# Lightning attention into a gated feed-forward: two-block tiles with one bank and one cosine for two w_in slices, fewer homes, and a last block in one piece

## The chip, the cores and the metric

The kernel runs on one core of a Trainium2 chip. The metric is the device time of a run in microseconds (us), lower is better. The times of the kernel before are 202.65, 202.12 and 202.6 us, median 202.6. Engines are named as in the profile: PE (TensorE matmuls), PEld (its weight loads), DVE (VectorE), ACT (ScalarE), POOL (GpSimd), SP (SyncE, which issues most DMAs); a name with a small q (SPq, ACTq) is an engine's sequencer.

## The reference

Two computations in a row. First a linear attention with decay: for 4 batches and 8 heads, in blocks of 64 positions, `intra = (qb @ kb.T * Dmask) @ vb`, `inter = (qb * lam_pow) @ kv_state`, `out = intra + inter`, and the state is carried on, `kv_state = lam_block * kv_state + kb_dec.T @ vb`. Its output, put in token order, is `x` of 3072 tokens by 512. Then a feed-forward:

```python
h = x @ w_in            # 512 -> 2048
g = h * np.cos(h)
return (g @ w_out).astype(np.float32)   # 2048 -> 512
```

## The kernel before, in words

The 3072 tokens are 24 blocks of 128 tokens. They are cut into eight tiles of 4, 2, 2, 2, 2, 4, 4 and 4 blocks (`TILES`). Attention works on pairs of blocks (pair `pr` is blocks `2 pr` and `2 pr + 1`); the feed-forward works on tiles.

**Feed-forward of a tile.** w_in's 2048 columns are 16 slices of 128, numbered f. For each slice four matmuls (L753) sum into one PSUM bank `ps_h`, 512 columns wide for a tile of four blocks and 256 for one of two. ACT takes the cosine out of the bank (L759), DVE multiplies bank and cosine into `g` (L765, the gating product), and then the bank is free. For each block, 16 matmuls with w_out (L800) sum into a bank `ps_f`; ACT copies it out (L816) into a home `o_sb`, and a DMA stores it (L823 or L825). The last block, 23, is done in two pieces of 384 and 128 columns: 16 matmuls each; DVE copies the first piece and SP stores it, ACT copies the second and stores it itself.

**Attention in visits.** While PE does a tile's feed-forward, it turns for short visits to the attention of later pairs. A full visit for pair `pr` is one uninterrupted row on PE: values that need no turn (L491, `ps_o`, two banks), the scores of the next pair (L429, `ps_s`, two banks), its state update (L441, `ps_kv`, two banks, and PE writes them in turn, matmul by matmul), the other values (L491) and the carried part (L523). Between the first and the other values stands a one-element DVE copy out of `ps_o` (L508, tile `spare`; called the turn copy here); it waits until the first values are done, and the other values wait for it. After the visit DVE multiplies scores with the mask (`s_m`, L434) and sums states (`sum`, L447), and ACT casts states (`S`, L451) and the attention output (`xT`, L531).

**Banks and homes.** PSUM has eight banks, and everything above shares them; a bank is taken again once its last reader is through. Outputs of blocks 0 to 11 are held back in SBUF until the key transposes of pair 10 have been issued on SP (`HELD`), since the loads of q, k and v fill the DMA queues until then. Before, these twelve have homes of their own (`o_held`, 12 buffers, which earlier hold parts of the start), and other outputs have three (`o_sb`). Raw q, k and v of a block each take one of six buffers (`ld`).

**Order.** Every engine's order is written out by a planner: tasks have durations, dependencies and a priority, and each engine takes, among the tasks that could start, the one of best priority. The turn copy has a priority ahead of everything and may make DVE wait for it up to 0.45 us of planned time although another task could start (`look.worth`). What the planner assumes sets the order alone; on the chip each engine runs its row in that order and waits where it must.

Of the kernel before, what the change touches and what calls it, by code (L numbers as in the profile page):

```python
# [10 lines left out]
F32 = mybir.dt.float32  # L11
BF16 = mybir.dt.bfloat16
# [18 lines left out]
HELD = (10,) * 12  # L31

# [30 lines left out]
class Planner:  # L63


    LAT = {"PE": 0.2, "ACT": 0.06, "DVE": 0.08, "POOL": 0.1, "SP": 0.0, "DMA": 0.0, "SETUP": 0.0}

# [10 lines left out]
    def order(self):  # L78
# [5 lines left out]
        while todo:  # L84
# [24 lines left out]
            free[t.eng] = t.end  # L109
# [44 lines left out]
def kernel(  # L154
# [30 lines left out]
    BUFS = {"ld": 6, "qk": 3, "v_s": 6, "qkT": 3, "s_m": 4, "cos": 3, "o_sb": 3, "o_held": 12}  # L185
# [55 lines left out]
    unit = [MM(n * P, 4 * KF) + MM(DM, KF * n) + ATT * n for n in TILES]  # L241
# [356 lines left out]
    span_v = [consts.tile([P, H, 2, D], BF16, name=f"v_sp{x}") for x in range(SPANS)]  # L598

    def add_span(x):  # L600
# [109 lines left out]
    def add_span_state(s_t, prio):  # L710
# [21 lines left out]
        u.bank_frees = [[x]]  # L732

    h_last, o_last = {}, {}
    hid, closing = [], None

    def add_ffn(i):
        nb, n0 = TILES[i], first[i]
        cols = nb * P
        gate = {}  # L740

        for f in range(KF):
            gate[f] = []
            blocks = [(0, 2), (2, 4)] if i == 0 and f < SPLIT else [(0, nb)]
            for b0, b1 in blocks:
                pr = begins[i] + (f + b0 / 4 * SPLIT) * unit[i] / KF
                at = slice(b0 * P, b1 * P)
                n = (b1 - b0) * P

                def hidden(task, f=f, at=at, n=n):  # L750
                    t = bank(task.bank[0], [P, 4 * P], F32, "ps_h")
                    live["h", i, f, at.start] = t
                    return [nc.tensor.matmul(t[:, :n], lhsT=w_in_sb[:, kd, f * P:(f + 1) * P],  # L753
                                             rhs=live["xT", i][:, kd, at], start=(kd == 0), stop=(kd == KD - 1))
                            for kd in range(KD)]

                def cosine(_, f=f, at=at, n=n):
                    c = work.tile([P, 4 * P], F32, tag="cos", bufs=BUFS["cos"], name="cos")
                    nc.scalar.activation(c[:, :n], live["h", i, f, at.start][:, :n], AF.Sin, bias=halfpi)  # L759
                    live["c", i, f, at.start] = c  # L760

                def gated(_, f=f, at=at, n=n):
                    if ("g", i) not in live:
                        live["g", i] = work.tile([P, KF, 4 * P], BF16, tag="g", name="g")
                    return nc.vector.tensor_mul(live["g", i][:, f, at], live.pop(("h", i, f, at.start))[:, :n],  # L765
                                                live.pop(("c", i, f, at.start))[:, :n])

                h = pl.add("PE", MM(n, 4), [x for m in range(n0 + b0, n0 + b1) for x in Vo[m]] + [w_t["in", next(c for c in range(len(W_IN)) if f < sum(W_IN[:c + 1]))]],
                           hidden, pr, banks=1)
                a = pl.add("ACT", 0.21 + n * 0.000833, [h], cosine, pr, get="cos")  # L770
                d = pl.add("DVE", 0.12 + n * 0.00104, [a] + ([o_last[i - 2]] if i >= 2 else []), gated, pr)
                h.bank_frees = [[d]]
                a.frees = [d]
                gate[f].append(d)
                if i == 0 and f == KF - 3:
                    pace.append(d)
                h_last[i] = h
                h.many = True
                if i == 0:
                    hid.append(h)  # L780
        nonlocal closing
        nxt = unit[i + 1] if i + 1 < len(unit) else unit[i]
        U4 = 4
        for j in range(nb):
            last = n0 + j == NBLK - 1
            tag = "o_held" if n0 + j < len(HELD) or i == len(TILES) - 1 else "o_sb"
            cuts = [0, 3 * DM // 4, DM] if last else [0, DM]
            pieces = [slice(a, z) for a, z in zip(cuts, cuts[1:])]
            store = None
            for piece, part in enumerate(pieces):  # L790
                width = part.stop - part.start
                for f0, nf in [(0, 4), (4, 4), (8, 4), (12, 2), (14, 2)] if i == 0 else [(f, U4) for f in range(0, KF, U4)]:
                    pr = begins[i + 1] + (j + f0 / KF) * nxt / nb + piece
                    if i == 0 and f0 >= KF - U4:
                        pr = begins[i + 1] + (3.75 + 0.05 * j + 0.1 * (f0 - 12)) * nxt / nb

                    def project(task, j=j, f0=f0, nf=nf, piece=piece, part=part, width=width):
                        if f0 == 0:
                            live["f", i, j, piece] = bank(task.bank[0], [P, DM], F32, "ps_f")
                        return [nc.tensor.matmul(live["f", i, j, piece][:, :width], lhsT=live["g", i][:, f, j * P:(j + 1) * P],  # L800
                                                 rhs=w_out_sb[:, f, part], start=(f == 0), stop=(f == KF - 1))
                                for f in range(f0, f0 + nf)]

                    t = pl.add("PE", MM(width, nf), [x for f in range(f0, f0 + nf) for x in gate[f]] + (w_last[f0 - 12:f0 - 12 + nf] if f0 >= KF - U4 else [w_t["out", f0 * WCH // KF]]) + [store],
                               project, pr, banks=0 if f0 else 1)
                    if i == 0 and j == nb - 1:
                        closing = t
                    t.many = True
                    if f0 == 0:
                        head = t  # L810
                    store = t
                o_last[i] = store

                def project_out(_, eng, j=j, piece=piece, width=width, tag=tag):
                    o = live["o_sb", i, j, piece] = work.tile([P, DM], F32, tag=tag, bufs=BUFS[tag], name="o_sb")
                    return (nc.scalar.copy if eng == "ACT" else nc.vector.tensor_copy)(o[:, :width], live["f", i, j, piece][:, :width])  # L816

                def store_out(_, eng, j=j, piece=piece, part=part, width=width):
                    b, c = where(n0 + j)
                    r0 = b * S + c * P  # L820
                    if n0 + j < 2 * SPANS:
                        for s, h in enumerate(halves):
                            nc.sync.dma_start(out=out[r0 + s:r0 + P:2, :], in_=live["o_sb", i, j, piece][h])  # L823
                        return
                    (nc.scalar if eng == "ACT" else nc.sync).dma_start(  # L825
                        out=out[r0:r0 + P, part], in_=live["o_sb", i, j, piece][:, :width])

                eng, queue = ("DVE", "SP") if last and piece == 0 else ("ACT", "ACT" if last else "SP")
                e = pl.add(eng, 0.12 + width / 1060.0, [store], partial(project_out, eng=eng), begins[i + 1] + (j + 1) * nxt / nb,
                           get=tag)  # L830
                d = dma(queue, 1.2 if n0 + j < 2 * SPANS else 0.9, 1.7 if n0 + j < 2 * SPANS else 0.75, partial(store_out, eng=queue), n0 + j + 8, [e] + ([T[HELD[n0 + j], 1].issue] if n0 + j < len(HELD) else []), ordered=False)[1]
                e.frees = [d]
                head.bank_frees = [[e]]
# [136 lines left out]
```

## Time and profile before

| | |
|---|---|
| runs, median (lowest, highest) | 202.6 us (202.12, 202.65) |
| profiled execution, first to last instruction | 200.7 us |
| of a run outside that span, 202.6 - 200.7 | 1.9 us |
| PE busy | 192.9 us, 96% |
| DVE, ACT, POOL busy | 112.1, 117.1, 64.9 us |
| first matmul of the dense part, end of the last | 16.84, 197.62 us |
| granted clock of TensorE | 1.000 |

The span is that of one execution under the profiler. The profile has no time of that execution from the host's side, so the 1.9 us between its span and the median of the runs is taken as a constant. Durations of matmuls (379 ns for 512 columns) are from issue to the modelled end; the pace of matmuls in a row is read from stretches (24 in 5.18 us are 0.216 us each).

### The profile page before, as it was taken

To read this page: it belongs to the slowest core of one execution; us is meant where nothing else is said; L and a number is where in the kernel's file an instruction comes from. 1 tells how busy PE (TensorE), PEld (TensorE's weight loads), DVE (VectorE), ACT (ScalarE), POOL (GpSimd) and SP (SyncE) were. 2 spreads that over 40 slices of the span, in tenths; PEclk is the share of its full clock that TensorE was granted. 3 is DMA by queue.
4 is the path that set the end of the run, shared out by engine and by line. 5 is a ranking of instruction groups with operands and counts; after the bars stand their busy time and mean duration, and the time that the engine had idled before them with its cause. 6 is when DMAs were issued, how large, how long until landed. Compare 5 with 4: busy or idle time off the path is not lost.

```text
span 200.7 us, 5731 instructions
## 1 busy us (share of the span) xinstructions
PE 192.9 (96%) x2380; PEld 110.2 (55%) x2407; DVE 112.1 (56%) x211; ACT 117.1 (58%) x223; POOL 64.9 (32%) x86
## 2 busy tenths in 40 slices
PE   8899999999999999999999999999999999999993
PEld 2466444648758647858755454544445444444452
DVE  2978772448848816956745679565445453444001
ACT  5878771329769527939555878486356465344120
POOL 5893002284373645472636570006400000000000
DMA  5999999999899999998999997999611010111112
GB/s 163 303 191 202 205 196 239 289 221 177 203 218 214 184 241 201 214 213 184 191 207 220 245 206 183 318 314 223 162 56 54 3 52 6 49 52 52 52 63 97
DMA packets 96668, 34.46 MB, mean 172 GB/s; under 512 B 84738, under 2 KB 93186, under 8 KB 96642
## 3 DMA queue, kind: packets, MB, share of 16 engines
q1 hardware_dynamic: 89664, 29.83, 66.6%
q0 software_dynamic: 6832, 4.20, 14.5%
q8 instruction: 19, 0.31, 0.7%
q10 hardware_dynamic: 146, 0.07, 0.1%
q14 instruction: 7, 0.06, 0.1%
HBM read 27.26 MB, written 6.29 MB: 167 GB/s over the span
## 4 chain that ended last, share of the span: by engine, by line
PE 89%; DMA 6%; issue 1%; SPq 1%; POOL 1%; ACT 0%; POOLq 0%
PE ps_f L800 41%; PE ps_h L753 41%; DMA sp_f<-in_k_dram 3%; DMA w_in_sb<-in_moe_w_in_dram 3%; PE ps_o L491 2%; PE ps_o L523 2%; PE ps_kv L441 2%; PE ps_s L429 1%; SPq L260 1%; POOL k_sp L614 1%; PE ps_t L381 0%; PE ps_kv L718 0%; PE ps_x L491 0%; ACT o_sb L816 0%; POOLq L614 0%
## 5 line engine op out<-in xcount | busy, mean ns | idle before, releaser
L765 DVE TENSOR_TENSOR g<-ps_h,cos 128x256 bf16<-128x256 f32 (+1 forms) x133 | 70.6, 543 | 41.4 <-ACT cos L759 39.7
L800 PE MATMUL ps_f<-w_out_sb,g 128*128 128x512 bf16 (+2 forms) x380 | 87.6, 370 | 2.2 <-issue 1.6
L753 PE MATMUL ps_h<-xT,w_in_sb 128*128 128x256 bf16 (+1 forms) x525 | 88.8, 319 | 0.5 <-issue 0.2
L759 ACT ACTIVATE cos<-ps_h,halfpi 128x256 f32<-128x256 f32 (+1 forms) x133 | 72.0, 570 | 28.9 <-PE ps_h L753 28.3
L753 PEld LDWEIGHTS <-w_in_sb 128*128 128x128 bf16 x532 | 51.4, 98 | 32.9 <-DMA w_in_sb<-in_moe_w_in_dram 0.4
L800 PEld LDWEIGHTS <-g 128*128 128x128 bf16 x400 | 37.6, 98 | 40.4
L351 POOL TENSOR_TENSOR qk<-q_f,q_scale 128x512 bf16<-128x512 f32 x19 | 19.4, 1042 | 54.2 <-DMA q_f<-in_q_dram 54.2
L816 ACT COPY o_sb<-ps_f 128x512 f32<-128x512 f32 (+1 forms) x24 | 13.7, 574 | 22.6 <-PE ps_f L800 19.6
L359 POOL TENSOR_TENSOR v_s<-v_f,v_scale 128x512 bf16<-128x512 f32 x19 | 19.6, 1043 | 9.2 <-DMA v_f<-in_v_dram 5.4
L531 ACT CAST xT<-ps_o 128x512 bf16<-128x512 f32 x15 | 8.1, 589 | 13.6 <-PE ps_o L523 11.2
L434 DVE TENSOR_TENSOR s_m<-ps_s,mask 128x512 bf16<-128x512 f32 x20 | 12.9, 685 | 2.5 <-PE ps_s L429 2.0
L355 POOL CAST qk<-k_f 128x512 bf16<-128x512 f32 x18 | 11.0, 612 | 7.8 <-DMA k_f<-in_k_dram 7.8
L447 DVE TENSOR_TENSOR sum<-sum,ps_kv 128x512 f32<-128x512 f32 x15 | 10.2, 682 | 0.7
L451 ACT CAST S<-sum 128x512 bf16<-128x512 f32 x15 | 9.1, 618 | 1.0 <-DVE sum L447 0.9
L508 DVE COPY spare<-ps_o 1x1 f32<-1x1 f32 x8 | 1.2, 156 | 14.6 <-PE ps_o L491 14.6
L816 DVE COPY o_sb<-ps_f 128x384 f32<-128x384 f32 x1 | 0.6, 558 | 11.6 <-PE ps_f L800 11.6
L491 PEld LDWEIGHTS <-v_s 64*64 64x64 bf16 x320 | 4.2, 106 | 4.4 <-issue 4.0
L491 PE MATMUL ps_o<-s_m,v_s 64*64 64x64 bf16 x288 | 5.9, 197 | 0.0
L638 DVE TENSOR_TENSOR s_m_sp<-ps_s,mask_sp 128x512 bf16<-128x512 f32 x8 | 5.1, 685 | 1.3 <-PE ps_s L633 1.3
L892 PE MATMUL ps_idle<-const-float32-1.0 128*128 128x512 f32 (+1 forms) x6 | 4.8, 902 | 0.8 <-PEq L954 0.8
L523 PE MATMUL ps_o<-qkT,S 64*64 64x64 bf16 x304 | 5.0, 195 | 0.0
L441 PE MATMUL ps_kv<-v_s,qk 64*64 64x64 bf16 x288 | 4.8, 195 | 0.0
(77 smaller groups left out, 83.9 us busy)
## 6 DMA issues: line engine op xcount, KB each, us to landing
q_f<-in_q_dram SPq DMA_DIRECT2D x20, 256.0 KB, 3.9
k_f<-in_k_dram SPq DMA_DIRECT2D x20, 256.0 KB, 4.5
v_f<-in_v_dram SPq DMA_DIRECT2D x20, 256.0 KB, 4.5
out_dram<-o_sb SPq DMA_DIRECT2D x19, 256.0 KB, 2.8
w_out_sb<-in_moe_w_out_dram POOLq DMA_DIRECT2D x3, 512.0 KB, 13.6
sp_f<-in_q_dram SPq DMA_DIRECT2D x2, 512.0 KB, 4.9
sp_f<-in_k_dram SPq DMA_DIRECT2D x2, 512.0 KB, 5.4
w_in_sb<-in_moe_w_in_dram POOLq DMA_DIRECT2D x2, 512.0 KB, 9.1
```

The source lines that it names most:

```text
L351: return vec[e].tensor_mul(new_qk()[:, 0, :, s], live.pop(("q_f", 2 * pr + s)), q_scale[:, c, :].unsqueeze(2).to_broadcast([P, H, D]))
L355: return (nc.scalar.copy if early else nc.gpsimd.tensor_copy)(new_qk()[:, 1, :, s], live.pop(("k_f", 2 * pr + s)))
L359: return vec[e].tensor_mul(live["v_s", 2 * pr + s], live.pop(("v_f", 2 * pr + s)), v_scale[:, c, :].unsqueeze(2).to_broadcast([P, H, D]))
L434: return nc.vector.tensor_mul(t, live["s", pr][s], mask.unsqueeze(1).to_broadcast([P, H, D]))
L447: return nc.vector.tensor_add(new, live["sum", pr, 0] if half else live["sum", pr - 1, 1], live["kv", pr][half])
L451: return nc.scalar.copy(new_S(pr, half), live["sum", pr, half])
L491: yield lambda h=h: nc.tensor.matmul(o[halves[h % 2], h // 2], lhsT=live["v_s", n0 + s][m, h, :], rhs=live["s_m", n0 + s][m, h, :], start= ...
L753: return [nc.tensor.matmul(t[:, :n], lhsT=w_in_sb[:, kd, f * P:(f + 1) * P], rhs=live["xT", i][:, kd, at], start=(kd == 0), stop=(kd == KD ...
L759: nc.scalar.activation(c[:, :n], live["h", i, f, at.start][:, :n], AF.Sin, bias=halfpi)
L765: return nc.vector.tensor_mul(live["g", i][:, f, at], live.pop(("h", i, f, at.start))[:, :n], live.pop(("c", i, f, at.start))[:, :n])
L800: return [nc.tensor.matmul(live["f", i, j, piece][:, :width], lhsT=live["g", i][:, f, j * P:(j + 1) * P], rhs=w_out_sb[:, f, part], start= ...
L816: return (nc.scalar.copy if eng == "ACT" else nc.vector.tensor_copy)(o[:, :width], live["f", i, j, piece][:, :width])
```

## The change

Five things, and a large part of the diff that is not run (`FAST` is an empty list, so `project_pairs` and `add_w_sums` are never called).

- In tiles of two blocks, slices f and f+8 go into the two halves of one bank: eight matmuls of 256 columns, then one cosine and one gating product of 512 columns for both. Tiles of four blocks keep a bank for each slice, in the order 0, 8, 1, 9 and so on; w_out matmuls of a block come in the order f = 0-3, 8-11, 4-7, 12-15.
- `ld` goes from six to four buffers for each of q, k and v.
- All outputs share eleven homes (`o`) in place of 12 + 3. With the outputs of blocks 0 to 10 held, the twelfth output (block 11) has a home only when the stores of block 0 have landed.
- Block 23 is one piece of 512 columns, copied by ACT and stored by SP.
- Some tiles of the start move to other buffers, and the planner lets an engine start its next task 0.05 to 0.1 us before the planned end of the last (`TAIL`), with slightly longer cosines and gating products.

```diff
+    TAIL = {"ACT": 0.1, "DVE": 0.09, "POOL": 0.05}
-            free[t.eng] = t.end
+            free[t.eng] = t.end - self.TAIL.get(t.eng, 0.0)
-    BUFS = {"ld": 6, "qk": 3, "v_s": 6, "qkT": 3, "s_m": 4, "cos": 3, "o_sb": 3, "o_held": 12}
+    BUFS = {"ld": 4, "qk": 3, "v_s": 6, "qkT": 3, "s_m": 4, "cos": 3, "o": 11, "cmb": 2, "SA": 2, "E": 2}
...
+        if i == 0:
+            groups = [([f], b, (f + b[0] / 4 * SPLIT) / KF) for f in range(KF) for b in ([(0, 2), (2, 4)] if f < SPLIT else [(0, nb)])]
+        elif nb == 4:
+            groups = [([f], (0, nb), (2 * (f % HF) + f // HF) / KF) for x in range(HF) for f in (x, x + HF)]
+        else:
+            groups = [([x, x + HF], (0, nb), 2 * x / KF) for x in range(HF)]
...
+                return [nc.tensor.matmul(t[:, x * n:(x + 1) * n], lhsT=w_in_sb[:, kd, f * P:(f + 1) * P],
+                                         rhs=live["xT", i][:, kd, at], start=(kd == 0), stop=(kd == KD - 1))
+                        for x, f in enumerate(fs) for kd in range(KD)]
...
+                nc.scalar.activation(c[:, :m], live["h", key][:, :m], AF.Sin, bias=halfpi)
...
+                g = h_tile()[:, fs[0]:fs[-1] + 1:HF, at]
+                x = lambda t: t[:, :m].rearrange("p (f n) -> p f n", f=len(fs))
+                return nc.vector.tensor_mul(g, x(live.pop(("h", key))), x(live.pop(("c", key))))
...
-            cuts = [0, 3 * DM // 4, DM] if last else [0, DM]
...
+            for f0, nf in [(0, 4), (4, 4), (8, 4), (12, 2), (14, 2)] if i == 0 else [(0, 4), (8, 4), (4, 4), (12, 4)]:
...
-                eng, queue = ("DVE", "SP") if last and piece == 0 else ("ACT", "ACT" if last else "SP")
+            e = pl.add("ACT", 0.6, [store], project_out, begins[i + 1] + (j + 1) * nxt / nb, get="o")
```

**What moves, on DVE: tile 5 (blocks 12 to 15), around the visit for pair 8.** Before, then with the change. `g` is a gating product, `spare` the turn copy of this visit, `sum` and `s_m` follow the visit.

```order
L765 TENSOR_TENSOR g<-ps_h,cos 128x512 x9
L508 COPY spare<-ps_o 1x1
L765 TENSOR_TENSOR g<-ps_h,cos 128x512 x2
L434 TENSOR_TENSOR s_m<-ps_s,mask 128x512 x2
L447 TENSOR_TENSOR sum_2788<-sum_2502,ps_kv 128x512
L765 TENSOR_TENSOR g<-ps_h,cos 128x512 x2
L447 TENSOR_TENSOR sum_2812<-sum_2788,ps_kv 128x512
```

```order
L828 TENSOR_TENSOR g<-ps_h,cos 128x512 x8
L514 COPY spare<-ps_o 1x1
L828 TENSOR_TENSOR g<-ps_h,cos 128x512 x2
L440 TENSOR_TENSOR s_m<-ps_s,mask 128x512
L453 TENSOR_TENSOR sum_2628<-sum_2371,ps_kv 128x512
L440 TENSOR_TENSOR s_m<-ps_s,mask 128x512
L453 TENSOR_TENSOR sum_2642<-sum_2628,ps_kv 128x512
```

PE enters this visit after 11 slices of the tile before (44 matmuls), and after 10 now (40); DVE has 9 gating products ahead of the turn copy before and 8 now. Two gating products stand behind it in both.

**On ACT: the copy of block 11's output.** `S` and `xT` belong to the attention; the first `o_sb` row shown is block 10's, and ten cosines later comes the visit above. Before, then with the change.

```order
L816 COPY o_sb<-ps_f 128x512
L531 CAST xT<-ps_o 128x4x128 x2
L451 CAST S_2504<-sum_2499 128x512
L816 COPY o_sb<-ps_f 128x512
L759 ACTIVATE cos<-ps_h,halfpi 128x512
L451 CAST S_2531<-sum_2502 128x512
L759 ACTIVATE cos<-ps_h,halfpi 128x512 x10
L531 CAST xT<-ps_o 128x4x128 x2
```

```order
L880 COPY o_sb<-ps_f 128x512
L537 CAST xT<-ps_o 128x4x128 x2
L457 CAST S_2369<-sum_2357 128x512
L457 CAST S_2380<-sum_2371 128x512
L822 ACTIVATE cos<-ps_h,halfpi 128x512 x10
L537 CAST xT<-ps_o 128x4x128 x2
L822 ACTIVATE cos<-ps_h,halfpi 128x512
L457 CAST S_2649<-sum_2628 128x512
L822 ACTIVATE cos<-ps_h,halfpi 128x512 x2
L457 CAST S_2669<-sum_2642 128x512
L822 ACTIVATE cos<-ps_h,halfpi 128x512 x3
L880 COPY o_sb<-ps_f 128x512
```

Block 11's copy, the second `o_sb` row in each, moves from ahead of the tile's first cosine to behind its sixteenth. PE finishes block 11's sum at the same place in both, so its bank stays taken through the whole of tile 5's w_in part and through the visit.

**On ACT: the end.** Before, then with the change.

```order
L816 COPY o_sb<-ps_f 128x512
L759 ACTIVATE cos<-ps_h,halfpi 128x512
L816 COPY o_sb<-ps_f 128x512 x3
L816 COPY o_sb<-ps_f 128x128
L825 DMA out_dram<-o_sb 128x128
```

```order
L880 COPY o_sb<-ps_f 128x512
L822 ACTIVATE cos<-ps_h,halfpi 128x512 x4
L880 COPY o_sb<-ps_f 128x512
L822 ACTIVATE cos<-ps_h,halfpi 128x512
L880 COPY o_sb<-ps_f 128x512 x4
```

The last copy is 512 columns wide in place of 128, and its store is issued by SP, which now has ten full stores as its last rows in place of nine and one of 384 columns. DVE's last row, the copy of 384 columns, is gone. All other rows on SP and POOL stand in the same order.

More of the change, by code (lines that the diff above doesn't have):

```diff
@@ L31 @@
 HELD = (10,) * 12
+FAST = []
+WSUM = [["DVE"] * 3 + ["POOL"] * 2, ["DVE"] * 3 + ["POOL"] * 2]
+SEQ = [[(n, (g,)) for g, x in enumerate(("52341", "34521")) for n in x] + [(n, (0, 1)) for n in "76"], [(n, (0, 1)) for n in "5234176"]]
 APART = [3, 11]
@@ L597 @@
     spans, span_deps = [], []
[L598 removed]
+    span_s = [consts.tile([P, 2, NP, 2, P], BF16, tag="wide", bufs=3, name=f"s_m_sp{x}") for x in range(SPANS)]
+    span_vs = consts.tile([P, SPANS, H, 2, D], BF16, tag="wide", bufs=3, name="v_sp")
+    span_v = [span_vs[:, x] for x in range(SPANS)]
     def add_span(x):
@@ L605, in add_span @@
         vec = {"DVE": nc.vector, "POOL": nc.gpsimd}
-        L = {name: work.tile([P, 2, H, D], BF16, tag="o_held", bufs=BUFS["o_held"], name=f"{name}_sp{x}") for name in ("q", "k")}
+        L = {"q": work.tile([P, 2, H, D], BF16, tag="o", bufs=BUFS["o"], name=f"q_sp{x}")}
+        homes = work.tile([P, 3, 2 * DM], BF16, tag="cmb", bufs=BUFS["cmb"], name=f"span{x}")
+        L["k"] = homes[:, 0].rearrange("u (s h d) -> u s h d", s=2, h=H)
         L["v"] = span_v[x].rearrange("u h s d -> u s h d")
-        L.update({name: work.tile([P, 2, NP, P], BF16, tag="o_held", bufs=BUFS["o_held"], name=f"{name}_sp{x}") for name in ("qT", "kT")})
-        L["s_m"] = consts.tile([P, 2, NP, 2, P], BF16, name=f"s_m_sp{x}")
+        L.update({name: homes[:, i].rearrange("u (s p t) -> u s p t", s=2, p=NP) for i, name in ((1, "qT"), (2, "kT"))})
+        L["s_m"] = span_s[x]
         spans.append(L)
@@ L737, in add_ffn, with held @@
+    def held(n):
+        return [T[HELD[n], 1].issue] if n < len(HELD) else []
     def add_ffn(i):
+        nonlocal closing
         nb, n0 = TILES[i], first[i]
+        np_ = nb // 2
         cols = nb * P
         gate = {}
[L742 to L780, printed above, removed]
@@ new lines, in h_tile @@
+        def h_tile():
+            if ("g", i) not in live:
+                live["g", i] = work.tile([P, KF, cols], BF16, tag="g", name="g")
+            return live["g", i]
+        if i == 0:
[4 more added lines that the diff above has]
+            groups = [([x, x + HF], (0, nb), 2 * x / KF) for x in range(HF)]
@@ L781, in add_ffn, with project_plain @@
+        nxt = unit[i + 1] if i + 1 < len(unit) else unit[i]
+        if i not in FAST:
+            project_plain(i, gate, nxt)
+        else:
+            project_pairs(i, gate, nxt)
+    def project_plain(i, gate, nxt):
         nonlocal closing
-        nxt = unit[i + 1] if i + 1 < len(unit) else unit[i]
-        U4 = 4
+        n0, nb = first[i], TILES[i]
         for j in range(nb):
-            last = n0 + j == NBLK - 1
-            tag = "o_held" if n0 + j < len(HELD) or i == len(TILES) - 1 else "o_sb"
-            cuts = [0, 3 * DM // 4, DM] if last else [0, DM]
-            pieces = [slice(a, z) for a, z in zip(cuts, cuts[1:])]
@@ L789, in add_ffn @@
             store = None
[L790 to L807, printed above, removed]
-                    t.many = True
[L809 to L826, printed above, removed]
-                eng, queue = ("DVE", "SP") if last and piece == 0 else ("ACT", "ACT" if last else "SP")
[L829 to L833, printed above, removed]
@@ new lines, in project_plain, with project @@
+            for f0, nf in [(0, 4), (4, 4), (8, 4), (12, 2), (14, 2)] if i == 0 else [(0, 4), (8, 4), (4, 4), (12, 4)]:
+                pr = begins[i + 1] + (j + f0 / KF) * nxt / nb
+                if i == 0 and f0 >= KF - 4:
+                    pr = begins[1] + (3.75 + 0.05 * j + 0.1 * (f0 - 12)) * nxt / nb
+                def project(task, j=j, f0=f0, nf=nf):
+                    if f0 == 0:
+                        live["f", i, j] = bank(task.bank[0], [P, DM], F32, "ps_f")
+                    return [nc.tensor.matmul(live["f", i, j], lhsT=live["g", i][:, f, j * P:(j + 1) * P],
+                                             rhs=w_out_sb[:, f], start=(f == 0), stop=(f == KF - 1))
+                            for f in range(f0, f0 + nf)]
+                t = pl.add("PE", MM(DM, nf), [x for f in range(f0, f0 + nf) for x in gate[f]] + (w_last[f0 - 12:f0 - 12 + nf] if f0 >= KF - 4 else [w_t["out", f0 * WCH // KF]]) + [store],
+                           project, pr, banks=0 if f0 else 1)
+                if i == 0 and j == nb - 1:
+                    closing = t
+                closed[0] = t
+                t.many = True
+                if f0 == 0:
+                    head = t
+                store = t
@@ new lines, in project_plain, with project_out, store_out @@
+            o_last[i] = store
+            def project_out(_, j=j):
+                o = live["o", i, j] = work.tile([P, DM], F32, tag="o", bufs=BUFS["o"], name="o_sb")
+                return nc.scalar.copy(o, live["f", i, j])
+            def store_out(_, j=j):
+                b, c = where(n0 + j)
+                r0 = b * S + c * P
+                if n0 + j >= 2 * SPANS:
+                    nc.sync.dma_start(out=out[r0:r0 + P], in_=live["o", i, j])
+                    return
+                for s, h in enumerate(halves):
+                    nc.sync.dma_start(out=out[r0 + s:r0 + P:2, :], in_=live["o", i, j][h])
```

202 lines of the change are left out of this document (198 added, 4 removed).

## The prediction

> **What bounds the kernel now.** I read the busy times first, then the chain that ended last, then the waits, then busy time by stretch, and the timeline last.
>
> ```profile
> PE 192.9 (96%) x2380; PEld 110.2 (55%) x2407; DVE 112.1 (56%) x211; ACT 117.1 (58%) x223; POOL 64.9 (32%) x86
> PE 89%; DMA 6%; issue 1%; SPq 1%; POOL 1%; ACT 0%; POOLq 0%
> 101.34 5.18 PE ps_f L800 x24
> 190.50 7.12 PE ps_f L800 x48
> PE ps_f L800 <- issue: 1.6, 10, 0.2
> ACT cos L759 <- PE ps_h L753: 28.3, 57, 1.6
> DVE g L765 <- ACT cos L759: 39.7, 56, 2.5
> ```
>
> PE is the bound: 96% busy and 89% of the chain. ACT and DVE are busy little more than half of the time and stand waiting for PE, not the other way round: cosines waited 28.3 us for PE's sums, while PE's longest gap ahead of a w_out matmul is 0.2 us, with no engine named ("issue"). The pace of a dense row is 5.18 / 24 = 0.216 us for 512 columns. The chain ends with PE, at 190.50 + 7.12 = 197.62, and a copy and a store behind it.
>
> ```profile
> 45.00:58.00 13.00, 12.79 (x211) 9.37 (x212) 10.21 (x23) 10.38 (x26) 5.94 (x8) 1.00 0.96 202
> 58.00:75.00 17.00, 16.74 (x227) 11.10 (x219) 9.88 (x23) 10.62 (x25) 9.15 (x10) 1.00 1.22 210
> 75.00:90.00 15.00, 14.63 (x300) 10.93 (x292) 10.96 (x25) 9.78 (x22) 8.54 (x11) 1.00 1.17 215
> 90.00:110.00 20.00, 19.63 (x351) 13.15 (x353) 12.25 (x27) 13.02 (x29) 9.87 (x12) 1.00 1.05 200
> 110.00:125.00 15.00, 14.89 (x190) 7.41 (x191) 11.65 (x19) 12.34 (x20) 6.38 (x7) 1.00 1.07 212
> ```
>
> These are the stretch, its length, and the busy us of PE, PEld, DVE, ACT and POOL, then granted clock, DMA share and GB/s. The first four hold the tiles of two blocks, where most of the edit lies, the fifth the visit that I come to below. PE is idle 0.21 + 0.26 + 0.37 + 0.37 = 1.21 us of the first four, at a full clock (1.00). So whatever the change saves on ACT and DVE can give at most that, and whatever it makes PE wait is added to the end in full, for nothing behind PE has room to take it up.
>
> **The two-slice banks: nothing.** What they remove, by form (out<-in, count, busy us and mean ns, idle before):
>
> ```profile
> L759 ACT ACTIVATE cos<-ps_h,halfpi 128x256 f32<-128x256 f32 x74 | 31.8, 477 | 4.8 <-PE ps_h L753 4.7
> L759 ACT ACTIVATE cos<-ps_h,halfpi 128x512 f32<-128x512 f32 x59 | 40.4, 687 | 24.1 <-PE ps_h L753 23.6
> L765 DVE TENSOR_TENSOR g<-ps_h,cos 128x256 bf16<-128x256 f32 x74 | 30.3, 424 | 9.8 <-ACT cos L759 8.5 <-DMA v_f<-in_v_dram 0.7
> L765 DVE TENSOR_TENSOR g<-ps_h,cos 128x512 bf16<-128x512 f32 x59 | 40.5, 691 | 31.7 <-ACT cos L759 31.2
> ```
>
> Four tiles of sixteen slices lose 64 small cosines for 32 large: 64 x 0.477 - 32 x 0.687 = 8.5 us less on ACT. On DVE it is 64 x 0.424 - 32 x 0.691 = 5.0 us. PE does the same matmuls of 256 columns, eight in a row in place of four and four. Since PE does not wait for either engine there, I take 0 of the 1.21 us; idle time in crumbs of at most 0.2 us with no engine behind it is not theirs. The price is latency: a tile's last gating product is now done 0.687 + 0.691 = 1.38 us after PE's last sum, against 0.90. It fills slices 7 and 15 at once, and the w_out matmuls of a block take slices 4 to 7 as their third group of four; two groups, 8 x 0.216 = 1.73 us, stand ahead. That covers 1.38 with 0.3 us to spare; where it does not, the loss is at most the added latency, 0.48 us a tile.
>
> The Trainium skill, Perfetto Trace Analysis, section Optimizing Scalar/DVE Operations, says that larger operations raise throughput where the engine is saturated, and that where Scalar and Vector are not saturated but cause bubbles elsewhere, breaking instructions up lets work finish sooner. That speaks against the joining; the 58% and 56% above are the unsaturated case, though PE's rows show no bubble of theirs yet. By it each of the four tiles would lose up to the 0.48 us added; by the rows they lose none (D below).
>
> **Fewer loads buffers, other span homes, planner costs: nothing.** Four `ld` buffers are enough, because the loads of a pair are issued behind the transposes of the pair before in both rows of SP; nothing is moved past another queue's work. The start is bound by w_in's arrival.
>
> **Eleven homes: a wait on PE.** This is the first term. The visit for pair 8, in tile 5, before:
>
> ```profile
> 118.20 0.69 DVE L765 TENSOR_TENSOR g<-ps_h,cos 128x512 bf16<-128x512 f32 x1 [0.17 <-ACT cos L759]
> 118.35 0.69 ACT L759 ACTIVATE cos<-ps_h,halfpi 128x512 f32<-128x512 f32 x1 [0.18 <-PE ps_h L753]
> 119.10 0.32 PE L491 MATMUL ps_o<-s_m,v_s 64*64 64x64 bf16 x16
> 119.25 0.43 PE L429 MATMUL ps_s<-qkT 64*64 64x64 bf16 x32
> 119.43 3.04 SPq L823 DMA_DIRECT2D out_dram<-o_sb  x4
> 119.48 0.16 DVE L508 COPY spare<-ps_o 1x1 f32<-1x1 f32 x1 [0.58 <-PE ps_o L491]
> 119.50 0.59 PE L441 MATMUL ps_kv<-v_s,qk 64*64 64x64 bf16 x32
> 119.67 1.29 DVE L765 TENSOR_TENSOR g<-ps_h,cos 128x512 bf16<-128x512 f32 x2
> 120.54 1.68 PE L753 MATMUL ps_h<-xT,w_in_sb 128*128 128x512 bf16 x6
> ```
>
> The visit writes six banks: two each of `ps_o`, `ps_s` and `ps_kv`. The two gating products that stand behind the turn copy hold two more. That is eight, and PE goes through without a wait. With the change block 11's copy stands behind the tile's sixteenth cosine, since its home is that of block 0's output, whose store leaves only at 119.43. Its bank is still taken at the visit: nine wanted, eight there. The one that is short is the second `ps_kv` bank, which must be that of the ninth slice, whose gating product stands behind the turn copy. DVE keeps its row: the cosine of 118.35 was done at 119.04, but its product began at 119.67, only after the copy. And the copy waits for the visit's own first matmuls. So PE, which could start the second `ps_kv` matmul at about 119.52, must wait for one gating product, 119.67 + 0.69 = 120.36, and the step from DVE to PE.
>
> ```profile
> 4.83 1.29 DVE L614 TENSOR_TENSOR q_sp<-sp_f,q_sp 128x512 bf16<-128x512 f32 x2 [0.81 <-DMA sp_f<-in_q_dram]
> 5.58 0.17 PEld L622 LDWEIGHTS <-q_sp 128*128 128x128 bf16 x3 [1.74 <-DVE q_sp L614]
> ```
>
> Two products in 1.29, the first of 0.69: it ends at 5.52, and PE's load begins at 5.58, 0.06 later. So PE goes on at 120.42: the wait is 120.42 - 119.52 = **0.9 us**. The visit comes one slice earlier in the tile now (after 10), which moves DVE, ACT and PE together and leaves these distances. Behind the waiting matmul on PE's row stand the rest of the visit and all that follows. Bounds: 0, if the bank turns out not to be short, and 120.96 + 0.06 - 119.52 = 1.5, if both products must be through. I take 0.9, since one bank is short and not two.
>
> Block 11's own copy should then not be late. Its home needs block 0's two stores; SP issues them from 119.43 on at 3.04 / 4 = 0.76 us each, the second at 120.2.
>
> ```profile
> out_dram<-o_sb SPq DMA_DIRECT2D x2, 128.0 KB, 3.4
> ```
>
> Landed (median, from issue) 3.4 us later: 123.6. The sixteenth cosine comes after six more slices: a visit begun at 119.10 - 0.86 = 118.24, lasting 1.43 + 0.9, then 6 x 0.864 and a cosine, together 126.4. There are 2.8 us in hand.
>
> **The last block whole: the second term.**
>
> ```profile
> 194.77 2.91 SPq L825 DMA_DIRECT2D out_dram<-o_sb  x2
> 196.76 0.56 DVE L816 COPY o_sb<-ps_f 128x384 f32<-128x384 f32 x1 [11.55 <-PE ps_f L800]
> 197.65 0.27 ACT L816 COPY o_sb<-ps_f 128x128 f32<-128x128 f32 x1 [2.91 <-PE ps_f L800]
> 197.94 0.38 ACTq L825 DMA_DIRECT2D out_dram<-o_sb  x1
> L800 PE MATMUL ps_f<-w_out_sb,g 128*128 128x384 bf16 x16 | 2.8, 326 | 0.0
> L800 PE MATMUL ps_f<-w_out_sb,g 128*128 128x128 bf16 x16 | 1.1, 219 | 0.0
> L816 ACT COPY o_sb<-ps_f 128x512 f32<-128x512 f32 x23 | 13.4, 587 | 19.7 <-PE ps_f L800 16.7 <-remote 2.9
> out_dram<-o_sb SPq DMA_DIRECT2D x1, 256.0 KB, 2.0
> out_dram<-o_sb SPq DMA_DIRECT2D x1, 192.0 KB, 1.9
> out_dram<-o_sb ACTq DMA_DIRECT2D x1, 64.0 KB, 1.6
> ```
>
> Before, the 384 columns were copied and their 192 KB sent under PE's cover: copied by 197.32, while PE still worked to 197.62. Behind PE were only a copy of 0.27 and a store of 64 KB that lands 1.6 us after its issue. Now the copy is one of 0.587 (+0.32) and the store one of 256 KB, 2.0 us (+0.40; the row is block 22's). PE gains a crumb: 48 matmuls took 7.12, of which 0.16 is the last one's modelled end beyond its pace (0.219 - 0.216 / 4); 16 of 512 columns are 3.46, so the two pieces took 3.50 against 3.46 for one whole block (-0.04). Sum: +0.32 + 0.40 - 0.04 = **+0.68 us**. From below +0.28 (a store's size costs nothing at the end), from above +1.1 (landing 0.4 later still, as long again as the step from 64 to 256 KB). I take the rows of the end of the same trace.
>
> The Trainium skill, DMA: Bandwidth & Descriptors, section Issuing engines are not separate DMA queues, says that starting transfers from several engines saves only the sequencer's time, since all run on the same 16 DMA engines. By that alone one whole store would cost no more than two pieces, and the end would be +0.28; the rows here say that the earlier piece was sent ahead, under PE, which one store cannot be.
>
> **Sum.** 0.9 + 0.68 = 1.58: a span of 200.7 + 1.6 = 202.3. The profiled span lies 1.9 us below the median of 202.6; I keep those 1.9, so the run is **204.2 us**.
>
> **Rivals.**
> - **A, the wait is covered** (or a bank is free that I count as taken), and only the end grows: 202.6 + 0.68 = 203.3. For it: the bank tally is worked out, no row shows it. Against: DVE's row at 119.67 shows the product behind the copy plainly.
> - **B, two such waits.** Block 0's stores land late, since the DMA share is above 1 while they run (1.07); block 11's copy slips beyond 126.4, and the visit after this one finds the same bank taken and waits 0.9 again: 202.6 + 0.68 + 1.8 = 205.1. It decides if a store takes over 3.4 + 2.8 = 6.2 us to land. Against: twice the median.
> - **C, the other side: the lighter ACT and DVE take away PE's idle time in the two-block tiles.** Its place is 45 to 110 us, its price at most -1.21, and it needs the visit to go through without a wait: 202.6 + 0.68 - 1.2 = 202.1, not slower than before. It decides from 0.7 us of gain on. For it: 8.5 and 5.0 us less work; PE is idle there more than twice as much as in the fifth stretch (1.21 of 65 us is 1.9%, 0.11 of 15 is 0.7%). Against: no row names ACT or DVE behind a gap of PE.
> - **D, the joined gating comes too late** for the third group in all four two-block tiles: 4 x 0.48 on top of the forecast, 206.1. It decides if a cosine begins over 0.3 us behind its sum. Against: ACT's row at 118.35 had idled 0.18 us and was free for its sum.
> - **The change does less than it says:** `FAST` is empty, so its new projection of pairs never runs. That is in the forecast.
>
> **How the numbers follow.** Forecast 0.62; A 0.16; B 0.11; C 0.08; D 0.03. A measurement of this kernel tells some 0.3% from no change, 0.6 us: 202.0 to 203.2. The forecast, B and D are slower; A lies at the upper edge, so I give half of it to no change; C is spread over no change and faster, with a little more for faster from what I don't see at the start. Faster 0.07, same 0.15, slower 0.78. The forecast's own bounds are 202.6 + 0.9 + 0.28 = 203.8 and 202.6 + 1.5 + 0.68 = 204.8. To leave out no more than 2 in 10 the range reaches down to A less the 0.3 us by which runs scatter, and up to B: 203.0 to 205.1.
>
> **What would show it.** In the changed profile: in tile 5 the visit's second `ps_kv` matmul begins some 0.9 us after the first, with a wait for `g` named on PE or an "issue" gap of that size, and PE's busy share in that stretch falls. If `ps_kv` runs through in 0.6 us, A or C holds. Block 11's copy begins at about 126.4; much later is B. In the two-block stretches PE's idle time stays near 1.2 us; under 0.5 is C. A wait ahead of the first block's w_out matmuls of slices 12 to 15 would say that the joined gating came too late. Behind the last matmul: a copy of 0.59, SP's issue 0.02 us later, a landing 2.0 us after that. The forecast is wrong if PE's last matmul ends before 198.0 or after 199.2.

## The result

| | before | changed |
|---|---|---|
| runs, median (lowest to highest) | 202.53 us (202.12 to 202.65) | 204.5 us (204.15 to 204.86) |
| ratio, 95% interval | | 1.0097, 1.008 to 1.0113 |
| profiled execution, span | 200.7 us | 202.7 us |
| PE, DVE, ACT busy | 192.9, 112.1, 117.1 us | 194.1, 106.8, 111.3 us |
| PE's last matmul ends | 197.62 us | 198.87 us |
| from there to the end of the span | 3.1 us | 3.8 us |

The change is 1.97 us slower, 0.97%. DVE and ACT have become lighter by 5.3 and 5.8 us, and the time did not go down. The page of the changed kernel, busy times and the chain:

```profile
PE 194.1 (96%) x2365; PEld 110.3 (54%) x2391; DVE 106.8 (53%) x178; ACT 111.3 (55%) x191; POOL 64.5 (32%) x86
PE 92%; DMA 2%; issue 1%; DVE 1%; ACT 1%; DVEq 0%
```

PE is the bound as before, but DVE and ACT now have a share of the chain. The view of what PE waited for (total us, times, longest) names the two places:

```profile
PE ps_kv L447 <- DVE g L828: 0.7, 1, 0.7
PE ps_h L816 <- ACT xT L537: 0.2, 1, 0.2
```

Neither row exists in the kernel before. **The first** is in the visit for pair 8, in the timeline of the changed kernel:

```profile
118.84 0.32 PE L497 MATMUL ps_o<-s_m,v_s 64*64 64x64 bf16 x16
...
118.95 0.69 ACT L822 ACTIVATE cos<-ps_h,halfpi 128x512 f32<-128x512 f32 x1 [0.18 <-PE ps_h L816]
...
119.21 0.16 DVE L514 COPY spare<-ps_o 1x1 f32<-1x1 f32 x1 [0.58 <-PE ps_o L497]
...
119.24 0.21 PE L447 MATMUL ps_kv<-v_s,qk 64*64 64x64 bf16 x1
...
119.40 1.29 DVE L828 TENSOR_TENSOR g<-ps_h,cos 128x512 bf16<-128x512 f32 x2
...
120.14 0.44 PE L447 MATMUL ps_kv<-v_s,qk 64*64 64x64 bf16 x31 [0.70 <-DVE g L828]
...
120.99 1.25 PE L816 MATMUL ps_h<-xT,w_in_sb 128*128 128x512 bf16 x4
...
126.96 0.58 ACT L880 COPY o_sb<-ps_f 128x512 f32<-128x512 f32 x1
```

One `ps_kv` matmul goes, 31 wait for a gating product that starts behind the turn copy: 119.40 + 0.69 = 120.09, and PE goes on at 120.14. The row says 0.70, since it counts from the modelled end of the single matmul. The whole visit took 120.99 - 118.84 = 2.15 us, against 120.54 - 119.10 = 1.44 before: **0.71 us**. Block 11's copy, the last row, came at 126.96.

**The second** is at the visit for pair 4, between the tile of blocks 6 and 7 and that of blocks 8 and 9. The changed kernel, then the kernel before:

```profile
76.96 1.07 ACT L537 CAST xT<-ps_o 128x512 bf16<-128x512 f32 x2 [2.38 <-DVE s_m L440]
...
77.04 0.81 PE L863 MATMUL ps_f<-w_out_sb,g 128*128 128x512 bf16 x3 [0.16 <-issue]
...
77.47 0.10 PEld L816 LDWEIGHTS <-w_in_sb 128*128 128x128 bf16 x1
...
78.09 2.13 PE L816 MATMUL ps_h<-xT,w_in_sb 128*128 128x256 bf16 x18 [0.24 <-ACT xT L537]
```

```profile
75.93 1.07 ACT L531 CAST xT<-ps_o 128x512 bf16<-128x512 f32 x2 [2.38 <-DVE s_m L434]
...
76.01 1.67 PE L800 MATMUL ps_f<-w_out_sb,g 128*128 128x512 bf16 x7 [0.16 <-issue]
...
77.52 2.67 PE L753 MATMUL ps_h<-xT,w_in_sb 128*128 128x256 bf16 x23
```

After a visit ACT casts the attention's output to `xT`, two casts in 1.07 us, and the next tile's first w_in matmul needs both. Before, PE had eight w_out matmuls to do meanwhile (7 in the record; one is missing); now it has four. The last of these was issued at 77.04 + 2 x 0.216 = 77.47 and could have been followed at 77.69; the w_in matmul went at 78.09, right behind the casts (78.03). That is **0.40 us**.

**The end.** The timeline of the changed kernel and its transfers (KB, us to landing):

```profile
193.74 5.13 PE L863 MATMUL ps_f<-w_out_sb,g 128*128 128x512 bf16 x23
...
198.90 0.58 ACT L880 COPY o_sb<-ps_f 128x512 f32<-128x512 f32 x1 [2.87 <-PE ps_f L863]
```

```profile
out_dram<-o_sb SPq DMA_DIRECT2D x2, 256.0 KB, 2.0
```

Here stand a copy of 0.58 and a landing of 2.0, against 0.27 and 1.6 before. From PE's last matmul to the end of the span 202.7 - 198.87 = 3.83, against 200.7 - 197.62 = 3.08: **0.75 us** more.

**The start** gives the rest. Both kernels' PE does the same work up to the transposes of the first pair that follows the start. In the kernel before, then in the changed one:

```profile
35.01 0.61 PE L381 MATMUL ps_t<-ident,qk 128*128 128x128 bf16 x8
```

```profile
35.21 0.55 PE L387 MATMUL ps_t<-ident,qk 128*128 128x128 bf16 x7
```

That is 0.20 us (the second row ends at 35.6 us and leaves out the eighth transpose). The sum is 0.20 + 0.40 + 0.71 - 0.04 (one block whole on PE) + 0.75 = 2.02, against 2.0 between the spans.

### The profile page after: what moved, and what is told of

It reads as the page before. It is cut to its first block, busy times and chain, and to the rows that moved or that the text cites. A ratio compares the mean times of both kernels' runs of the same rounds, so it can differ in the third digit from the quotient of the medians.

```text
span 202.7 us, 5609 instructions
## 1 busy us (share of the span) xinstructions
PE 194.1 (96%) x2365; PEld 110.3 (54%) x2391; DVE 106.8 (53%) x178; ACT 111.3 (55%) x191; POOL 64.5 (32%) x86
## 4 chain that ended last, share of the span: by engine, by line
PE 92%; DMA 2%; issue 1%; DVE 1%; ACT 1%; DVEq 0%
PE ps_h L816 41%; PE ps_f L863 40%; DMA sp_f<-in_q_dram 2%; PE ps_o L497 2%; PE ps_t L632 1%; PE ps_o L529 1%; PE ps_kv L447 1%; PE ps_s L435 1%; PE ps_s L643 1%; PE ps_idle L1105 1%; PE ps_o L669 1%; PE ps_kv L656 1%; ACT xT L537 1%; PE ps_t L387 0%; DVE q_sp L624 0%
## 5 line engine op out<-in xcount | busy, mean ns | idle before, releaser
L828 DVE TENSOR_TENSOR g<-ps_h,cos 128x512 bf16<-128x512 f32 (+1 forms) x101 | 66.3, 664 | 47.5 <-ACT cos L822 45.0
L863 PE MATMUL ps_f<-w_out_sb,g 128*128 128x512 bf16 x363 | 86.3, 379 | 2.3 <-issue 1.7
L822 ACT ACTIVATE cos<-ps_h,halfpi 128x512 f32<-128x512 f32 (+1 forms) x101 | 66.5, 666 | 37.9 <-PE ps_h L816 36.7
L863 PEld LDWEIGHTS <-g 128*128 128x128 bf16 x384 | 36.5, 98 | 41.0
L880 ACT COPY o_sb<-ps_f 128x512 f32<-128x512 f32 x24 | 14.0, 592 | 19.6 <-PE ps_f L863 16.9
L440 DVE TENSOR_TENSOR s_m<-ps_s,mask 128x512 bf16<-128x512 f32 x20 | 13.6, 686 | 3.0 <-PE ps_s L435 2.2
L635 ACT COPY span<-ps_t 128x512 bf16<-128x512 bf16 x8 | 4.7, 585 | 2.1 <-PE ps_t L632 1.9
```

The lines of the kernel that those rows point to most:

```text
L440: return nc.vector.tensor_mul(t, live["s", pr][s], mask.unsqueeze(1).to_broadcast([P, H, D]))
L822: nc.scalar.activation(c[:, :m], live["h", key][:, :m], AF.Sin, bias=halfpi)
L828: return nc.vector.tensor_mul(g, x(live.pop(("h", key))), x(live.pop(("c", key))))
L863: return [nc.tensor.matmul(live["f", i, j], lhsT=live["g", i][:, f, j * P:(j + 1) * P], rhs=w_out_sb[:, f], start=(f == 0), stop=(f == KF ...
L880: return nc.scalar.copy(o, live["f", i, j])
```

## The experiments

Times are medians; the ratio is to the kernel before, on the same chip, with its 95% interval. Differences to the changed kernel (1.0097) are differences of such ratios times 202.5 us, and each is uncertain by some 0.45 to 0.5 us, by 0.6 us in the experiment with the dummies.

### Twelve homes again

```diff
-    BUFS = {"ld": 4, "qk": 3, "v_s": 6, "qkT": 3, "s_m": 4, "cos": 3, "o": 11,
+    BUFS = {"ld": 4, "qk": 3, "v_s": 6, "qkT": 3, "s_m": 4, "cos": 3, "o": 12,
```

> The changed kernel with twelve homes for outputs in place of eleven, so that block 11's copy stands ahead of tile 5's cosines again. Theory (block 11's bank is the ninth that is wanted at the visit for pair 8): PE's wait for a gating product of 0.70 us inside that visit is gone, ps_kv runs through in about 0.6 us, and the time is 0.75 us less than the changed kernel's 204.5: 203.75. Rival (the wait comes from the visit's place, one slice earlier than before, after 10 slices in place of 11): the visit still stands after 10 slices here, the wait stays, and the time is 204.5.

203.43 us, ratio 1.0047 (1.0032 to 1.0062): 1.0 us less than the changed kernel, where 0.75 was expected. In the traces the visit is 0.85 us shorter (1.30 in place of 2.15):

```profile
118.77 0.32 PE L497 MATMUL ps_o<-s_m,v_s 64*64 64x64 bf16 x16
...
119.14 0.16 DVE L514 COPY spare<-ps_o 1x1 f32<-1x1 f32 x1 [0.58 <-PE ps_o L497]
...
119.17 0.49 PE L447 MATMUL ps_kv<-v_s,qk 64*64 64x64 bf16 x32
...
119.33 1.29 DVE L828 TENSOR_TENSOR g<-ps_h,cos 128x512 bf16<-128x512 f32 x2
...
120.07 1.68 PE L816 MATMUL ps_h<-xT,w_in_sb 128*128 128x512 bf16 x7
```

The visit stands after the same ten slices, both gating products still stand behind the turn copy, and all 32 `ps_kv` matmuls run through in 0.49 us. So it is the held bank and not the visit's place.

### Eleven homes in the kernel before

```diff
-    BUFS = {..., "o_sb": 3, "o_held": 12}
+    BUFS = {..., "o_sb": 3, "o_held": 11}
```

> The kernel before with one edit: eleven homes for held outputs in place of twelve; two more visits (pairs 10 and 9's order of casts) shift by crumbs. Theory: block 11's copy goes behind tile 5's cosines, the visit for pair 8 is one bank short there too, PE waits 0.7 us for a gating product, and the time is 0.75 more than before: 203.3. Rival (it takes the joined banks or the new order of slices as well to make the wait): 202.5.

203.22 us, ratio 1.0033 (1.0017 to 1.0049), 0.73 us more by the medians. The wait is there, in the same form:

```profile
119.52 0.21 PE L441 MATMUL ps_kv<-v_s,qk 64*64 64x64 bf16 x1
...
119.68 1.29 DVE L765 TENSOR_TENSOR g<-ps_h,cos 128x512 bf16<-128x512 f32 x2
...
120.43 0.44 PE L441 MATMUL ps_kv<-v_s,qk 64*64 64x64 bf16 x31 [0.70 <-DVE g L765]
```

One home less makes the wait alone, without joined banks or another order of slices.

### A gating product ahead of the turn copy

```diff
-            look.worth = 0.45
+            look.worth = 0.0 if pr == 8 else 0.45
```

> The changed kernel, with DVE not holding back for the turn copy of the visit for pair 8: nine gating products stand ahead of that copy in place of eight, one behind it; eleven homes as in the changed kernel, so the bank of block 11 is still taken. Theory (the visit's second ps_kv matmul waits for the ninth gating product, which DVE held behind the turn copy): the product now starts when its cosine is done, 0.6 us earlier, PE's wait falls from 0.75 to about 0.3 us, time 204.05. Rival (the bank that is waited for is another's, block 11's or block 10's): the wait stays 0.75, time 204.5.

204.11 us, ratio 1.008 (1.0064 to 1.0095): 0.3 us less. The visit:

```profile
119.01 0.69 DVE L828 TENSOR_TENSOR g<-ps_h,cos 128x512 bf16<-128x512 f32 x1 [0.17 <-ACT cos L822]
...
119.05 0.32 PE L497 MATMUL ps_o<-s_m,v_s 64*64 64x64 bf16 x16
...
119.45 0.75 PE L447 MATMUL ps_kv<-v_s,qk 64*64 64x64 bf16 x32
...
119.74 0.16 DVE L514 COPY spare<-ps_o 1x1 f32<-1x1 f32 x1
...
120.67 1.02 PE L816 MATMUL ps_h<-xT,w_in_sb 128*128 128x512 bf16 x4
```

The ninth product now ends at 119.70, `ps_kv` takes 0.75 us in place of the 0.49 of an undisturbed row, and the visit 1.62. The wait has shrunk to about 0.3 us and follows the ninth product's end, which shows whose bank is waited for. The difference in time, 0.3 us, is within its uncertainty; the trace carries this verdict.

### The last block: two pieces in the changed kernel, one piece in the kernel before

```diff
+            cuts = [0, 3 * DM // 4, DM] if last else [0, DM]
+                eng, queue = ("DVE", "SP") if last and piece == 0 else ("ACT", "ACT" if last else "SP")
```

> The changed kernel with its last block in two pieces of 384 and 128 columns again (DVE copies and SP stores the first, ACT copies and stores the second). Theory (behind the last matmul stand a longer copy, +0.32, and a larger store, +0.40): from PE's last matmul to the end of the span it is 3.1 us in place of 3.8, and the time is 0.7 less, 203.8. Rival (a store's size costs nothing at the end, only the copy does): 0.3 less, 204.2.

```diff
-            cuts = [0, 3 * DM // 4, DM] if last else [0, DM]
+            cuts = [0, DM]
-                eng, queue = ("DVE", "SP") if last and piece == 0 else ("ACT", "ACT" if last else "SP")
+                eng, queue = "ACT", "SP"
```

> The kernel before with one edit: the last block in one piece of 512 columns, copied by ACT and stored by SP. Theory: +0.7, 203.2, with 3.8 us from PE's last matmul to the end of the span in place of 3.1. Rival (only the copy counts): +0.3, 202.8.

203.69 us, ratio 1.0064 (1.0046 to 1.0083), 0.7 less than the changed kernel; and 203.27, ratio 1.0034 (1.0006 to 1.0062), 0.7 more than the kernel before. The end of the second, timeline and chain:

```profile
197.48 0.59 ACT L816 COPY o_sb<-ps_f 128x512 f32<-128x512 f32 x1 [2.87 <-PE ps_f L800]
```

```profile
183.63 13.83 PE ps_f L800 x64
```

PE ends at 183.63 + 13.83 = 197.46 and the span at 201.3: 3.84 us, as in the changed kernel. In the trace of the first it is 3.2 us (PE ends at 198.51, the span at 201.7). The times alone do not exclude the rival's 0.3, which lies inside both intervals; the traces do, for the copy alone would leave 3.4. Size and issuing queue of the last store change together here, so what each of them costs is not shown.

### The visit for pair 4, four matmuls earlier

```diff
             v1 = pl.add("PE", 4 * QUART + SW, deps, values, pa(0.5), banks=2 + 2 * apart)
+            v1.worth = 0.1 if pr in (4, 7) else 0.0
```

> The changed kernel, with the planner told to let PE wait up to 0.1 us of planned time for the visits of pairs 4 and 7; eight w_out matmuls now stand between the visit for pair 4 and the w_in matmuls that need its xT, as in the kernel before, and four in the changed kernel. Theory (the changed kernel's PE waits 0.4 us at 77.7 us for ACT's cast to xT, because the visit slipped by four matmuls): that wait is gone, time 204.1. Rival (the gap there is a visit's usual crumb and no wait): 204.5.

204.01 us, ratio 1.0077 (1.006 to 1.0094): 0.4 us less, as expected, though the uncertainty reaches from nothing to more than twice that. The trace is plain: no wait for `xT`, eight w_out matmuls behind the visit and the w_in matmuls right behind them.

```profile
75.78 1.90 PE L864 MATMUL ps_f<-w_out_sb,g 128*128 128x512 bf16 x8
...
77.51 2.67 PE L817 MATMUL ps_h<-xT,w_in_sb 128*128 128x256 bf16 x23
```

The span of that profile, 202.7, is not shorter than the changed kernel's, but that execution was the slowest of five (205.23 us); the other four had spans of 202.1 and 202.2. The visits at 87 and 107 us take 0.2 us longer in it than in some other profiles (1.53 and 1.55 against 1.31 and 1.30 in the start experiment below). What makes such differences between executions is open.

### Joined banks alone

In the kernel before, only the two-block tiles' slices are joined, and their w_out order is changed:

```diff
+        else:
+            groups = [([x, x + KF // 2], (0, nb), 2 * x / KF) for x in range(KF // 2)]
...
+                g = live["g", i][:, fs[0]:fs[-1] + 1:KF // 2, at]
...
-else [(f, U4) for f in range(0, KF, U4)]:
+else [(0, 4), (8, 4), (4, 4), (12, 4)] if nb == 2 else [(f, U4) for f in range(0, KF, U4)]:
```

> The kernel before with one edit: tiles of two blocks put slices f and f+8 into one bank, with one cosine and one gating product for both, and take w_out in the order 0-3, 8-11, 4-7, 12-15. Theory: the joining itself gives nothing, since PE does not wait for ACT or DVE in these tiles, but it moves the visit for pair 4 four w_out matmuls later and so makes PE wait 0.4 us for xT: 202.9. Rival 1 (nothing for nothing): 202.5. Rival 2 (lighter ACT and DVE take away PE's idle time there): 201.7 or less.

203.02 us, ratio 1.0024 (1.0007 to 1.0041), 0.5 us more. The wait of the changed kernel stands in its trace, at the same place:

```profile
76.74 1.07 ACT L531 CAST xT<-ps_o 128x512 bf16<-128x512 f32 x2 [2.42 <-PE ps_o L523]
...
77.87 2.34 PE L757 MATMUL ps_h<-xT,w_in_sb 128*128 128x256 bf16 x20 [0.24 <-ACT xT L531]
```

So the joining, with its order of w_out, is enough to bring the wait for `xT`. It does so by the order that the planner writes: four w_out matmuls more stand ahead of this visit and four fewer behind it. Why the planner puts them there is not shown; that its planned times shift by crumbs is an argument from its rules.

Then the same, with that visit kept early by the edit of the section before this one:

> The kernel before with joined banks in the tiles of two blocks and nothing else of the change, and the visit for pair 4 kept eight w_out matmuls ahead of the w_in matmuls that need its xT. Theory (joining costs by that visit alone, and gives nothing): 202.5, and PE's idle time from 45 to 110 us is that of the kernel before, 1.2 us within 0.3. Rival (the joining helps, hidden so far by the wait for xT): 202.1 or less. Rival (the joining costs by its latency, a wait ahead of w_out matmuls): 202.9 or more.

202.43 us, ratio 0.9992 (0.9981 to 1.0003): no difference. No wait for `xT` is left in its trace, and the records show PE idle 1.17 us from 45 to 110 us, as expected (what these idle times are is told below). Joining as such gives at most 0.4 us and costs at most 0.1 us, by the ends of the interval.

### The dummies of the start

```diff
             cols = min(int((us - 0.04) * 1200.0) // 64 * 64, 4 * P)
+            cols = {128: 256, 512: 384}.get(cols, cols)
```

> The changed kernel with the sizes that the kernel before had for PE's dummy matmuls at the start (256, 384, 256 and 384 columns in place of 128, 512, 128 and 448). Theory (the shorter dummies leave PE slow: four transposes take 0.61 us in place of 0.40 up to 9.6 us, and the first w_in matmul stands at 14.62 in place of 14.12): the transposes take 0.40 again and the time is 0.2 us less, 204.3. Rival (the slow stretch starts ahead of the first of these dummies, with a float32 dummy that took 2.08 in place of 1.93 us, and is chance of the run, as is the load that landed 0.17 later): no change, 204.5, and slow starts show up in some kernels of both kinds.

204.32 us, ratio 1.0084 (1.0057 to 1.0111): not to be told from the changed kernel. The number is the theory's 204.3, but the theory is not borne out. With the larger dummies four transposes still take 0.61 us at the start; and in the kernel before with its last block whole, whose start is that of the kernel before, they do so too. Its timeline:

```profile
3.34 2.08 PE L892 MATMUL ps_idle<-const-float32-1.0 128*128 128x512 f32 x2
...
5.51 0.61 PE L622 MATMUL ps_t<-ident,q_sp 128*128 128x128 bf16 x4
```

With the changed kernel's own dummies the start can be fast, as in the timeline of the early-visit experiment:

```profile
3.34 2.00 PE L1106 MATMUL ps_idle<-const-float32-1.0 128*128 128x512 f32 x2
...
5.58 0.40 PE L633 MATMUL ps_t<-ident,q_sp 128*128 128x128 bf16 x4 [0.23 <-DVE q_sp L625]
```

The slow stretch ends anywhere from 5 to 10 us, in kernels of both kinds. A late start goes with a long one: in the two profiles in which it lasted beyond 9 us, the changed kernel's and that of the turn copy, the first w_in matmul stands at 14.62 and 14.68 us, in the other ten at 14.06 to 14.19 (here at 14.10). Both of the two had the smaller dummies, and so had four of the ten, so that these lengthen it at times is not excluded.

### All undone at once

Twelve homes, two pieces and the early visit together, in the changed kernel:

> The changed kernel with all three of its losses undone at once: twelve homes, the last block in two pieces, and the visits for pairs 4 and 7 with eight w_out matmuls behind the former; joined banks, four load buffers and the new slice order stay. Theory (the three are the whole loss: 0.75 + 0.7 + 0.4): 204.5 - 1.85 = 202.65, no different from the kernel before (202.5). Rival 1 (something else in the change costs too): 203.1 or more. Rival 2 (freed of these, the lighter ACT and DVE give something): 202.0 or less.

202.24 us, ratio 0.9993 (0.9979 to 1.0007): the kernel before, within what can be measured. Its start has the changed kernel's dummies. Neither wait is left in its trace. So the three account for the loss, and what stays of the change (joined banks, four load buffers, the order of slices, other span homes) gives at most 0.4 us and costs at most 0.15 us together, by the ends of the interval.

## Why the prediction was right

It said 204.2 us in a range of 203.0 to 205.1, slower; measured were 204.5. The forecast case came about in both of its terms, and a third loss of 0.40 us was not in it. That the number came so near is luck in part: in the spans the two terms measure 0.71 + 0.71 = 1.42 us where 1.58 was forecast, and this hides 0.16 of the 0.60 us that the third loss and the later start brought.

**The wait at the visit for pair 8, predicted 0.9.** Mechanism and place are as told: the trace names the gating product behind the turn copy, and three edits (one home more, one less, the product ahead of the copy) move the wait as the theory says. The second `ps_kv` matmul went at 120.14 where it would have gone at about 119.26, so 0.88 late; but the visit grew by only 0.71 against the kernel before, since that one's visit was not at its shortest: 1.44 us, where it takes 1.30 with twelve homes in the changed kernel. In the trace of before its `ps_kv` row took 0.59 us in place of 0.49; why is not shown. The term should have been taken against the visit of the trace and not against a visit without any wait. Rival A, the covered wait, is out.

**The last block whole, predicted +0.68.** Measured 0.71 in the trace (0.75 behind the last matmul, less the 0.04 of one whole block) and 0.7 in two experiments. The terms are as forecast: a copy of 0.58 and a landing of 2.0. The rule that several issuing engines save only the sequencer's time (the Trainium skill, DMA: Bandwidth & Descriptors, Issuing engines are not separate DMA queues) would have made it 0.28; the measurement decides for the forecast. What was lost is an early start: in the kernel before, most of the block is copied and sent while PE still works.

**The two-slice banks, predicted at nothing.** Right for what was weighed: the latency is covered, D did not happen (no wait for `g` ahead of a w_out matmul stands among PE's waits), and the advice to break instructions up (the Trainium skill, Perfetto Trace Analysis, Optimizing Scalar/DVE Operations) finds no bubble to cure. Wrong for what was left out. The step that failed is the term itself, put at nothing after weighing busy time and latency alone: it did not ask which visits the joining moves. The prediction looked at one moved visit, that for pair 8, whose move does "leave these distances". The visit for pair 4 was moved too, four matmuls later, and its distance is one that a move does change: the one from the visit to the next tile's first w_in matmul, which the 1.07 us of casts must fit into. The row that would have told it stands in the trace of before: `xT` done at 77.00, w_in at 77.52, so 0.52 in hand. The move takes 0.86 of it; 0.34 are lacking, and with the 0.06 from a producer's end to PE that is the 0.40 measured.

The saving that was weighed was also read too large on ACT. The 8.5 us are counts times mean durations, and cosines of 256 columns overlap: 74 of them at 0.477 are 35.3 us, but kept ACT busy 31.8. By busy time it is 64 x 31.8 / 74 - 32 x 40.4 / 59 = 5.6 us, and the cosines' busy time did fall from 72.2 to 66.5. No time hung on it.

**Rival B** fell: block 11's copy came at 126.96, that is 126.4 and the 0.6 by which its visit came later than assumed, and the next visit found its banks: its `ps_kv` row took 0.49 us.

**Rival C** had no ground at all. The idle time of 1.21 us that gave it its price is no idle time. Busy us by stretch in the kernel before with its last block whole, whose order on PE is that of the kernel before in these stretches:

```profile
45.00:58.00 13.00, 13.00 (x215) 9.36 (x213) 10.14 (x23) 10.38 (x25) 7.04 (x9) 1.00 1.18 214
58.00:75.00 17.00, 17.00 (x227) 11.13 (x225) 9.97 (x23) 10.49 (x25) 9.94 (x12) 1.00 1.17 237
75.00:90.00 15.00, 15.00 (x292) 10.82 (x283) 10.90 (x25) 9.92 (x22) 8.20 (x9) 1.00 1.18 229
90.00:110.00 20.00, 20.00 (x353) 13.19 (x352) 12.19 (x27) 13.05 (x29) 9.79 (x12) 1.00 1.08 201
```

PE is busy without a gap. This trace has all 384 w_out and 532 w_in matmuls on record; that of before has 380 of 400 and 525 of 532. What is missing there is often the first matmul behind a visit, as in the "x7" of eight above, and such a hole reads as 0.16 us of "issue"; one inside a row reads as 0.05.

**The start, predicted unchanged.** The 0.20 us by which the profiled execution was later there go with the slow stretch of PE that lasted beyond 9 us in it; whether that is chance of the execution is not settled. They are in the span and not surely in the median. Nor was the start of that execution bound by w_in's arrival: the chain that ended last runs through PE from 8.5 us on, where that of before waits for w_in up to 16.79.

## What to carry to other kernels

Where one engine was dense, lightening the others gave nothing that could be measured, and a buffer saved can cost: what holds a late output's home holds its PSUM bank, and a bank that is one short waits for an in-order engine that may have been told to do something else first. When an order is planned, check every visit that moved against what comes next on the dense engine, not only the one that stands out; slack is to be compared with the step of the move. And before an idle crumb becomes a term, see whether it is a missing record.

## What was not expected of the hardware

PE begins slower than it goes on, for a time that differs from execution to execution: four transposes take 0.61 us up to somewhere between 5 and 10 us, then 0.40, and a dummy of 512 columns 0.63 in place of 0.38, while the profile gives a granted clock of 1.00 throughout. In the changed kernel's windows of the start:

```profile
2.00:5.00 3.00, 3.00 (x6) 1.00 (x4) 0.29 (x2) 1.83 (x7) 1.43 (x5) 1.00 0.88 254
5.00:7.00 2.00, 1.66 (x11) 0.90 (x10) 1.80 (x3) 1.62 (x4) 1.79 (x2) 1.00 1.15 348
7.00:9.60 2.60, 2.52 (x30) 1.53 (x29) 2.40 (x5) 1.75 (x3) 1.68 (x3) 1.00 1.35 297
```

The Trainium skill (TensorE: Matmul & The Clock Gate, Part 1) tells of a gate that lets PE run at half rate until a window of some 3.4 us was busy, and of windows that run freely of the kernel's start; that the end of the slow stretch varies agrees with it. Its length does not fit so easily: PE was busy 3.00 + 1.66 + 2.52 = 7.18 of the 7.6 us of these rows and was still slow at 9.1 us. The clock column does not show the gate, so whether the slow stretch is its work is open.
